# Threshold attention and routed attention on one core: crosswise scoring of tail tiles, halved subtractions and a new list

## The chip, the core and the metric

The kernel runs on one core of a Trainium2 chip. The metric is the device time in microseconds (us) of one execution, as the median of several runs; lower is better. The engines are TensorE (PE, its weight loads PEld), VectorE (DVE), ScalarE (ACT), GpSimd (POOL) and SyncE (SP, which issues transfers). The accumulation memory that TensorE writes has eight banks.

## The reference

Two attentions stand one behind the other. The first takes 8 batches of 8 heads, 576 positions and head size 64, and keeps of each row of scores only what lies within `tau` of the row's maximum:

```python
scores = scale * np.matmul(q, k.transpose(0, 1, 3, 2))
thresh = np.max(scores, axis=-1, keepdims=True) - tau
scores = np.where(scores >= thresh, scores, -1000000000.0)
...
return np.matmul(attn, v).astype(np.float32)
```

Its output, heads side by side (512 wide), is the input of a layer of four experts. Each expert projects it to queries, keys and values of width 64, does causal attention over 576 positions, projects back to 512, and each position sums its two best experts with gate weights. Everything is float32.

## The kernel before

**Tiling.** The 576 positions are four tiles of 128 rows (`R` = 4) and a tail of 64. Heads and experts go in pairs: 32 pairs of heads, and for each of 8 batches two pairs of experts. In a pair one head lies in partitions 0 to 63 and the other in 64 to 127, so that TensorE multiplies for both at once, each in one half of its rows. A float32 operand is split into a high part and the rest (`HHL`: three products instead of one). So an operand has a copy (hi) and a subtraction (lo).

**First attention, for each pair of heads** (`load`, `prep`, `scores`, `attnv`). Keys and queries are loaded (5 and 4 transfers), transposed and split in `prep` (lines 278 to 293). For pairs 1 to 5 (`NLO`) the transposed operand goes through a buffer in SBUF, so that GpSimd can do the subtraction (`flat_lo`, line 1077). For each tile `scores` (295) makes the products (`s_both`, 1091), the row minimum (keys are scaled by a negative number) with a copy out of the banks on VectorE (`s_min`, 1103), the exponential on ScalarE (`s_exp`, 1117), the masking product with its row sum on VectorE (`s_stt`, 1120), and transposes whose results are copied to SBUF (`pt`, `pa`; `out_t`, 1186). `attnv` multiplies by the values. The tail tile of a pair holds 64 rows of each head. `s_both` scores it like any other, 128 rows per head into two pairs of banks, of which half the partitions matter, and two `s_min` on 64 partitions each put both heads into one buffer of 128 rows.

**Second attention, for each batch** (`second`, 377): projections (`proj`), values, the gate, and for each pair of experts scores, exponentials and products. Queries and keys are split with `q_hi` (1299) and `q_lo` (1302). The tail of a pair of experts is one tile already: queries stand in a block-diagonal operand (`q2d`, 1305) and `s2_tail` (1394) contracts all 128 rows, then adds the causal mask by one more matmul.

**Crossing.** `crossing` (1253) lets the two row halves of TensorE add into the same pair of banks: in the first half of the work row half r writes bank r, in the second half bank 1 - r. In between, a tiny instruction on another engine (`fence`, 1269) waits for the last matmuls of the first half, and the first matmuls of the second half wait for it. Helper `crossed` (237) makes these three tasks; projections, values and outputs use it.

**Order.** All tasks are emitted in an order that stands in the code: `ORDER` gives each task its place, `BY` the engine where several can do it (for a copy from the banks 0 is ScalarE and 1 is VectorE; for a subtraction 0 is GpSimd and 1 VectorE; for a fence 0, 1, 2 are VectorE, ScalarE, GpSimd). Each engine works its tasks in this order. `plan` (131) walks through the list with estimated durations and picks buffers, banks and filler matmuls for the start; it does not change the order.

The copies, subtractions and fences that the profile lists stand in helpers: line 996 is a copy on ScalarE, 998 on VectorE, 1000 on GpSimd, 1004 every plain subtraction, 1020 every matmul, 1010 and 1167 the transposes, 1272 and 1274 the fences, 1105 `s_min`, 1118 `s_exp`, 1122 `s_stt`.

Of the kernel before, what the change touches and what calls it, by code (L numbers as in the profile page):

```python
# [25 lines left out]
R = 4  # L26
# [17 lines left out]
QUERIES = ((0, 0, 5, 0, 0), (0, WH, 4, 0, 1), (1, 0, 5, 0, 0), (1, WH, 4, 0, 1))  # L44
# [40 lines left out]
PAD, HALF, SLOW, FILL = 700.0, 8000.0, 3.5, 107.0  # L85
# [44 lines left out]

def plan(tasks, filler):
# [5 lines left out]
    moved = port = 0.0  # L137
    order = []
    for t in sorted(tasks, key=lambda t: t.place):
        e = t.by  # L140
        ready = BEGIN
        for d in t.deps:
            ready = max(ready, d.end + (SELF if t.engines == (d.by,) else LATE if t.engines == ("POOL",) else CROSS))
# [37 lines left out]


# [28 lines left out]
def work(K):  # L211
# [66 lines left out]
    def prep(n):  # L278
        ki, qi, dk, dq, dv = LD[n]
        PREP[n] = []  # L280
        for cls, src, tiles, d, scale, f in (("kk", ki, K.kis, dk, True, "k"), ("qq", qi, K.qis, dq, False, "q")):
# [4 lines left out]
            if raw:  # L286
                a = evac(W + 80 * scale, lambda e, g=g, raw=raw, scale=scale: K.in_raw(e, raw, g, scale), m, [], [g, raw], name=f"{f}r.{n}")
                h = moved(W, lambda e, buf=buf, raw=raw: K.flat_hi(e, buf, raw), [a], [], [raw, buf], name=f"{f}h.{n}")
                o = minus(W, lambda e, buf=buf, raw=raw: K.flat_lo(e, buf, raw), [h], [raw, buf], f"{f}l.{n}")
            else:  # L290
                h = evac(W + 80 * scale, lambda e, g=g, buf=buf, scale=scale: K.in_hi(e, buf, g, scale), m, [], [g, buf], name=f"{f}h.{n}")
                o = task("DVE", t_dve(W + 60 * scale), lambda g=g, buf=buf, scale=scale: K.in_lo(buf, g, scale), [h], [], [g, buf], name=f"{f}l.{n}")
            PREP[n] += [buf, [h, o]]

    def scores(n, s):
# [81 lines left out]
    def second(b):  # L377
# [8 lines left out]
        def proj(ep):  # L386
            q2, k2, q2d = Buf("q2"), Buf("k2"), Buf("q2d")
            qs, ks = [], []
            for i, (buf, l) in enumerate(((q2, qs), (k2, ks))):
# [5 lines left out]
                l += [h, minus(S, lambda e, buf=buf, rw=rw: K.q_lo(e, buf, rw), [h], [buf, rw], f"ql.{name}")]  # L395
# [23 lines left out]
        def score(t, ep, gd):  # L419
# [96 lines left out]
    for n in range(NPR):  # L516
# [13 lines left out]
BVL = ((3, 4), (2, 1, 0))  # L530
ORDER = {
    "warm": [
        638,
    ],
    "tau": [
        1, 12, 2,
# [967 lines left out]
```

## Time and profile before

| | |
|---|---|
| median of 3 runs | 855.32 us (853.39 to 855.62) |
| the profiled execution's own time | 853.47 us |
| its span, first to last instruction | 851.7 us |
| matmuls (PE), weight loads (PEld) | 14428 each |
| instructions on VectorE, ScalarE, GpSimd | 2296, 1341, 593 |
| moved by transfers | 43.15 MB |

The profile is of one execution. "x320" is a count, "752" after a comma a mean duration in ns, "idle before" the time that the engine stood still just before these instructions, with what ended it. A busy PE is not PE at its peak, since matmuls overlap and their ends are modelled.

### The profile page before, as it was taken

How to read it: one execution, taken by the hardware profiler on the slowest of the kernel's cores; microseconds unless marked ns; L12 is line 12 of the kernel's file. 1: busy time of each engine (PE TensorE's matmuls, PEld its weight loads, DVE VectorE, ACT ScalarE, POOL GpSimd, SP SyncE). 2: the span in 40 equal slices, each digit the busy share in tenths (PEclk: the TensorE clock that was granted, in tenths of full speed). 3: DMA queues.
4: the chain of work that ended last, by engine and by line, in shares of the span. 5: the costliest groups of instructions: out<-in, count | busy, mean ns of one | idle time of the engine just before them, and what ended most of it. 6: DMA issues, size and time to landing. Idle time of an engine off the chain costs nothing. (4 is left out here: it accounts for less than half of the span.)

```text
span 851.7 us, 34826 instructions
## 1 busy us (share of the span) xinstructions
PE 819.7 (96%) x14428; PEld 768.0 (90%) x14428; DVE 759.2 (89%) x2296; ACT 647.2 (76%) x1341; POOL 309.4 (36%) x593
## 2 busy tenths in 40 slices
PE   9888999999999999999999999999999999999998
PEld 7778998899989999899989999889998899988997
DVE  6999989989889989999989999999989989899564
ACT  5988768985788768987589866887678975778465
POOL 5658324521333224433243223442244233342332
PEclk9999999999999999999999999999999999999999
DMA  5333211112131211212121321122113122120002
GB/s 125 83 77 75 58 23 39 36 29 63 36 78 33 77 42 25 63 49 54 36 67 33 82 56 32 40 59 53 34 32 90 28 56 49 37 59 2 15 12 90
DMA packets 135117, 43.15 MB, mean 51 GB/s; under 512 B 130096, under 2 KB 130096, under 8 KB 134960
## 3 DMA queue, kind: packets, MB, share of 16 engines
q1 hardware_dynamic: 133744, 40.64, 19.5%
q8 instruction: 113, 1.85, 1.0%
q10 hardware_dynamic: 1216, 0.30, 0.2%
q14 instruction: 44, 0.36, 0.1%
HBM read 31.47 MB, written 9.44 MB: 48 GB/s over the span
## 5 line engine op out<-in xcount | busy, mean ns | idle before, releaser
L1105 DVE TENSOR_SCALAR_CACHE_REDUCE e<-ps 128x576 f32<-128x576 f32 (+1 forms) x320 | 233.2, 752 | 23.3 <-PE ps L1020 16.3
L1118 ACT ACTIVATE e<-e,sm 128x576 f32<-128x576 f32 x288 | 215.6, 771 | 39.0 <-DVE e L1105 35.9
L1122 DVE SCALAR_TENSOR_TENSOR e<-e,sm,e 128x576 f32<-128x576 f32 x256 | 221.1, 881 | 4.5 <-ACT e L1118 1.6
L996 ACT ACTIVATE pt<-ps 128x640 f32<-128x640 f32 (+3 forms) x247 | 154.0, 640 | 37.8 <-PE ps L1167 25.5
L1020 PE MATMUL ps<-kk,qq 64*128 64x288 f32 x1920 | 173.5, 304 | 4.1 <-DVE e L1105 1.1
L1020 PE MATMUL ps<-pt,vm 128*64 128x128 f32 (+1 forms) x1536 | 155.8, 258 | 0.0
L1020 PEld LDWEIGHTS ps<-kk,qq 64*128 64x128 f32 x1920 | 141.3, 185 | 11.9 <-DVE e L1105 3.0
L1020 PE MATMUL ps<-pa,vm 128*64 128x128 f32 x1024 | 135.7, 275 | 3.6 <-DVE e L1105 2.6
L1167 PE MATMUL ps<-ident,e 64*128 64x64 f32 x2624 | 127.0, 226 | 10.2 <-DVE e L1105 2.2
L1020 PEld LDWEIGHTS ps<-pt,vm 128*64 128x64 f32 x1536 | 131.1, 137 | 0.0
L1167 PEld LDWEIGHTS ps<-ident,e 64*128 64x128 f32 x2624 | 108.2, 138 | 22.5 <-DVE e L1105 4.8
L1020 PEld LDWEIGHTS ps<-pa,vm 128*64 128x64 f32 x1024 | 111.9, 137 | 8.5 <-DVE e L1105 3.4
L1020 PE MATMUL ps<-x,wh 64*128 64x288 f32 x1024 | 106.1, 295 | 0.0
L1020 PEld LDWEIGHTS ps<-x,wh 64*128 64x128 f32 x1024 | 84.6, 185 | 0.7 <-DVE e L1105 0.3
L996 ACT ACTIVATE pa<-ps 128x512 f32<-128x512 f32 x112 | 66.2, 593 | 17.4 <-PE ps L1167 16.5
L1020 PE MATMUL ps<-x,wl 64*128 64x288 f32 x512 | 79.1, 292 | 0.0
L1392 ACT ACTIVATE e<-e,sm 128x384 f32<-128x384 f32 (+3 forms) x128 | 71.0, 557 | 5.2 <-DVE sm L1387 5.0
L1412 POOL TENSOR_SCALAR e<-e,sm 128x256 f32<-128x256 f32 (+4 forms) x107 | 64.0, 607 | 26.5 <-DVE sm L1163 7.3
L1387 DVE CUSTOM_DVE_ANT_0 e<-ps,tri 128x384 f32<-128x384 f32 (+3 forms) x128 | 58.5, 483 | 8.4 <-PE ps L1020 7.3
L1020 PE MATMUL ps<-wh,x 64*128 64x260 f32 x640 | 64.6, 283 | 0.0
L1115 POOL TENSOR_TENSOR sm<-sm 128x2 f32<-128x2 f32 (+1 forms) x69 | 24.1, 351 | 105.3 <-DVE e L1105 80.4
L1000 POOL TENSOR_SCALAR iw<-sg 128x256 f32<-128x256 f32 (+1 forms) x61 | 25.7, 430 | 97.0 <-DVE sg L1130 56.9
(158 smaller groups left out, 1687.8 us busy)
## 6 DMA issues: line engine op xcount, KB each, us to landing
vm<-in_v_dram SPq DMA_DIRECT2D x64, 128.0 KB, 2.8
out_dram<-ob SPq DMA_DIRECT2D x32, 256.0 KB, 2.4
ki<-in_k_dram SPq DMA_DIRECT2D x96, 64.0 KB, 2.5
qi<-in_q_dram SPq DMA_DIRECT2D x62, 80.0 KB, 2.5
qi<-in_q_dram SPq DMA_DIRECT2D x62, 64.0 KB, 2.4
ki<-in_k_dram SPq DMA_DIRECT2D x32, 80.0 KB, 2.5
vt<-in_v_dram SPq DMA_DIRECT2D x128, 16.0 KB, 2.2
out_dram<-ob SPq DMA_DIRECT2D x8, 128.0 KB, 2.8
```

What stands on the lines that cost most here:

```text
L996: self.nc.scalar.activation(dst, src, AF.Copy)
L1000: self.nc.gpsimd.tensor_scalar(dst, src, 1.0, 0.0, op0=ALU.mult, op1=ALU.add)
L1020: return self.nc.tensor.matmul(out, x, y, start=first, stop=last)
L1105: self.nc.vector.tensor_scalar(self.sides(sc)[rows], self.dbank(s)[rows, :, :HS], 0.0, None, op0=ALU.add, op1=ALU.min, accum_out=self.smal ...
L1115: self.nc.gpsimd.tensor_tensor(m[:, 8 + j:8 + j + n], m[:, 2 * j:2 * (j + n):2], m[:, 2 * j + 1:2 * (j + n):2], op=ALU.add)
L1118: self.nc.scalar.activation(self.row(e), self.row(sc), AF.Exp, bias=self.small(sm)[:, 2 * j:2 * j + 1], scale=-1.0)
L1122: self.nc.vector.scalar_tensor_tensor(self.row(e), self.row(sc), self.small(sm)[:, 8 + j:9 + j], self.row(e), op0=ALU.is_le, op1=ALU.mult, ...
L1167: self.nc.tensor.transpose(self.ps[:, g.slot + h, c * D:(c + 1) * D], x, self.ident[sl, sl])
L1387: self.nc.vector.tensor_tensor_reduce(self.row(p2)[:, :w], self.dbank(g)[:, j, :w], self.tri[:, SM - w:], 1.0, FAR, op0=ALU.add, op1=ALU.m ...
L1392: self.nc.scalar.activation(p, p, AF.Exp, bias=m[:, 2 * j:2 * j + 1], scale=-1.0, accum_out=m[:, 4 + 2 * j:5 + 2 * j])
L1412: (self.nc.vector if e == "DVE" else self.nc.gpsimd).tensor_scalar(p, p, x, 0.0, op0=ALU.mult, op1=ALU.add)
```

## The change

The first attention's tail gets a query operand that is block-diagonal in its last 128 columns. To get it, the second head's last 64 positions are loaded with a transfer of their own (5 query transfers for a pair instead of 4), and two memsets instead of one put zeros beside the two tails. The tail is scored crosswise (`s_tail`) into one pair of banks, and one `s_min` on 128 partitions follows. `s2_tail` becomes a crossed group too, in 64-row halves, and the mask is added in both halves. `flat_lo` and `q_lo` are issued as two halves of the columns (320 + 320 and 288 + 288). There are 48 new fences (32 `fs`, 16 `fs2t`).

The planner compares the times at which VectorE and GpSimd hold their shared port, with the last few stretches of the other engine, instead of the last one. The constants HALF and one duration differ. All of `ORDER` and `BY` is new (5034 tasks for 4896).

In the engine choices these families change most: `pt` on VectorE 31 to 43 of 288; `pt2` 15 to 21 of 112; `v2` 5 to 0; `ob` 7 to 2; `qu` 6 to 4; `zh` 7 to 13; `thr` 48 to 55; scalings `p2s` 12 to 5; `xl` 15 to 18; halves of `q_lo` of the projections 14 of 64, where it was 6 of 32 whole ones. Fences on VectorE, ScalarE and GpSimd: 26, 27, 31 to 33, 46, 53.

```diff
-QUERIES = ((0, 0, 5, 0, 0), (0, WH, 4, 0, 1), (1, 0, 5, 0, 0), (1, WH, 4, 0, 1))
+QUERIES = ((0, 0, 5, 0, 0), (0, WH, 4, 0, 1), (1, 0, 5, 0, 0), (1, WH, 3, 0, 1), (1, SM, 1, R, 1))
...
-PAD, HALF, SLOW, FILL = 700.0, 8000.0, 3.5, 107.0
+PAD, HALF, SLOW, FILL = 700.0, 6200.0, 3.5, 107.0
...
+def hit(s, a, b):
+
+    if b <= a or s - JIT >= b or s + JIT <= a:
+        return 0.0
+    p = min(1.0, max(0.0, (a - s + JIT) / (2 * JIT)))
+    return max(0.0, soft(b - s) - soft(a - s) - (b - a) * p)
...
-            more = soft(at["POOL"] - start - 200.0)
-            port = start + more + lat - 177.0
+            more = sum(hit(start, a, z - 200.0) for a, z in theirs[-6:])
+            mine.append((start, start + more + lat - 177.0))
         elif e == "POOL":
-            more = soft(port - start)
+            more = sum(hit(start, a, z) for a, z in mine[-8:])
+            theirs.append((start + more, start + more + lat))
...
+def halves(n):
+    return slice(0, n // 2), slice(n // 2, n)
...
-                o = minus(W, lambda e, buf=buf, raw=raw: K.flat_lo(e, buf, raw), [h], [raw, buf], f"{f}l.{n}")
+                o = [minus(W // 2, lambda e, buf=buf, raw=raw, c=c: K.flat_lo(e, buf, raw, c), [h], [raw, buf], f"{f}l.{n}") for c in halves(W)]
...
-        bufs = [Buf("s") for _ in range(2)]
+        bufs = [Buf("s") for _ in range(nj)]
...
-        a = pe(6 * T_S, lambda: K.s_both(bufs, qq, kk, s), [*dk, *dq], [*bufs, *dict.fromkeys((sc, ee)), sm, sg], [qq, kk], "R", kind="S", name=f"s.{n}.{s}")
-        ms = []
-        for j in range(2):
-            x = j if s < R else 0
-            ms.append(task("DVE", (782, 80), lambda j=j, x=x: K.s_min(bufs[j], scs[x], sm, x, slice(0, P) if s < R else HEADS[j]), [a], [],
-                           [bufs[j], sc, sm], name=f"min.{n}.{s}"))
-        es = [task("ACT", (773, 101), lambda j=j: K.s_exp(scs[j], sm, ees[j], j), [ms[j]] if s < R else ms, [], [sc, sm, ee], name=f"exp.{n}.{s}")
+        takes = [*bufs, *dict.fromkeys((sc, ee)), sm, sg]
+        if s < R:
+            a = pe(6 * T_S, lambda: K.s_both(bufs, qq, kk, s), [*dk, *dq], takes, [qq, kk], "R", kind="S", name=f"s.{n}.{s}")
+        else:
+            a = crossed(3 * T_S, lambda y: K.s_tail(bufs[0], qq, kk, y), [*dk, *dq], takes, [qq, kk], bufs[0], f"s.{n}.{s}")
+        ms = [task("DVE", (782, 80), lambda j=j: K.s_min(bufs[j], scs[j], sm, j), [a], [], [bufs[j], sc, sm], name=f"min.{n}.{s}") for j in range(nj)]
+        es = [task("ACT", (773, 101), lambda j=j: K.s_exp(scs[j], sm, ees[j], j), [ms[j]], [], [sc, sm, ee], name=f"exp.{n}.{s}")
...
-                l += [h, minus(S, lambda e, buf=buf, rw=rw: K.q_lo(e, buf, rw), [h], [buf, rw], f"ql.{name}")]
+                l += [h, *[minus(S // 2, lambda e, buf=buf, rw=rw, c=c: K.q_lo(e, buf, rw, c), [h], [buf, rw], f"ql.{name}") for c in halves(S)]]
...
-                a = pe(f32r(6, HS) + 260, lambda: K.s2_tail(sb, q2d, k2), ks + dd, [sb, sm, pb], [q2d, k2], name=f"s2t.{name}")
+                a = crossed(f32r(3, HS) + 60, lambda y: K.s2_tail(sb, q2d, k2, y), ks + dd, [sb, sm, pb], [q2d, k2], sb, f"s2t.{name}")
...
+    "fs": [
+        26, 124, 220, 338, 458, 603, 756, 904, 1071, 1180, 1371, 1616, 1610, 1770, 1984, 2221, 2238, 2402, 2567, 2833, 2875, 3066, 3223, 3445, 3591, 3606, 3821, 4005, 4158, 4285,
+        4410, 4598,
...
+        692, 704, 805, 823, 1279, 1291, 1493, 1506, 1883, 1896, 2020, 2036, 2599, 2604, 2649, 2656, 3201, 3218, 3264, 3274, 3818, 3838, 3964, 3976, 4408, 4421, 4568, 4580, 4862,
+        4867, 4873, 4892,
+    ],
+    "fs2t": [
+        696, 819, 1290, 1500, 1887, 2021, 2600, 2654, 3206, 3266, 3824, 3974, 4412, 4570, 4863, 4886,
...
-        for t in self.kis + self.qis:
+        for t in self.kis:
             nc.vector.memset(t[ST:, R], 0.0)
+        for t in self.qis:
+            for j in range(2):
+                nc.vector.memset(t[ST:, R - j, j], 0.0)
...
+    def s_tail(self, s, qq, kk, y):
+
+        q, k = self.kq(qq), self.kq(kk)
+        self.crossing(HHL, y, s, lambda m, r, sl, hf, first, last: self.mm(
+            self.dbank(s)[:, hf, :HS], q[sl, m[0], SM:SM + P], k[sl, m[1], hf * HS:(hf + 1) * HS], first, last))
...
-        g = self.dbank(s)
-        for hf in range(2):
-            for i, (x, y) in enumerate(HHL):
-                self.mm(g[:, hf, :HS], self.q2ds[q2d.slot][:, x], self.q2(k2)[:, y, hf * HS:(hf + 1) * HS],
-                        i == 0, hf == 0 and i == 2)
-        self.mm(g[:, 1, HS - ST:HS], self.ident_b, self.mask2, False, True)
+    def s2_tail(self, s, q2d, k2, y):
+
+        g, q, k = self.dbank(s), self.q2ds[q2d.slot], self.q2(k2)
+
+        def mm(m, r, sl, hf, first, last):
+            x = self.mm(g[:, hf, :HS], q[sl, m[0]], k[sl, m[1], hf * HS:(hf + 1) * HS], first, last and hf == 0)
+            if hf and m is HHL[-1]:
+                x = self.mm(g[:, 1, HS - ST:HS], self.ident_b[sl], self.mask2[sl], False, last)
+            return x
+        self.crossing(HHL, y, s, mm)
```

The shown lists are the places of the fences of the first tails (`fs`), and of the two halves (`s2t`) and fences (`fs2t`) of the second tails. Between the two halves of a first tail the new list has other TensorE groups for 30 of the 32 pairs (transposes, scores, projections, outputs); for pairs 0 and 1 it has none.

## Rows read from the trace of the kernel before

**Rows 1.** The page: busy times of the engines; granted clock in 40 slices.

```profile
PE 819.7 (96%) x14428; PEld 768.0 (90%) x14428; DVE 759.2 (89%) x2296; ACT 647.2 (76%) x1341; POOL 309.4 (36%) x593
...
PEclk9999999999999999999999999999999999999999
```

**Rows 2.** Busy time by engine, sixteen 20 us stretches where VectorE is fullest, summed.

```profile
sum 320.00, PE 302.04 PEld 275.74 DVE 306.25 ACT 272.67 POOL 135.78; mean PE 43.15 PEld 39.39 DVE 43.75 ACT 38.95 POOL 19.40
```

**Rows 3.** Busy time by engine, all other stretches, summed.

```profile
sum 511.70, PE 499.12 PEld 476.95 DVE 439.88 ACT 365.14 POOL 163.90; mean PE 71.30 PEld 68.14 DVE 62.84 ACT 52.16 POOL 23.41
```

**Rows 4.** Groups by shape: the minimum on VectorE, and its accumulator read on 64 partitions.

```profile
L1105 DVE TENSOR_SCALAR_CACHE_REDUCE e<-ps 128x576 f32<-128x576 f32 x256 | 185.2, 751 | 17.1 <-PE ps L1020 13.8 <-ACT v L996 0.7 <-ACT rw L996 0.3
...
L1105 DVE TENSOR_SCALAR_CACHE_REDUCE e<-ps 64x576 f32<-64x576 f32 x64 | 48.2, 754 | 6.3 <-PE ps L1020 2.4 <-ACT pt L996 0.8 <-ACT ob L996 0.6
...
L1105 DVE DVE_READ_ACCUMULATOR e<-ps 64x1 f32 x64 | 5.0, 78 | 0.0
```

**Rows 5.** Busy time of line 1105 alone, in the stretches of rows 2, summed.

```profile
sum 320.00, DVE 96.09; mean DVE 13.73
```

**Rows 6.** Groups by shape: two copies out of the banks on VectorE.

```profile
L998 DVE COPY pt<-ps 128x640 f32<-128x640 f32 x17 | 13.8, 815 | 0.7 <-PE ps L1167 0.6
...
L998 DVE COPY ob<-ps 128x512 f32<-128x512 f32 x7 | 4.8, 688 | 3.7 <-PE ps L1020 3.4 <-issue 0.4
```

**Rows 7.** The masking product: group by shape, then its line's ns min/median/max.

```profile
L1122 DVE SCALAR_TENSOR_TENSOR e<-e,sm,e 128x576 f32<-128x576 f32 x256 | 221.1, 881 | 4.5 <-ACT e L1118 1.6 <-ACT sm L1113 0.8
...
L1122 DVE SCALAR_TENSOR_TENSOR e<-e,sm,e x256: 777/813/2185, 15.6 to 788.7; 128x576 f32<-128x576 f32 x128
```

**Rows 8.** Groups by shape: subtractions on GpSimd.

```profile
L1004 POOL TENSOR_TENSOR q<-rw,q 128x576 fp32r<-128x576 f32 x14 | 21.3, 1521 | 13.8 <-DVE sm L991 13.2 <-ACT q L996 0.4
...
L1004 POOL TENSOR_TENSOR x<-iv,x 128x256 fp32r<-128x256 f32 x21 | 16.7, 798 | 5.9 <-ACT x L996 3.6 <-DVE x L998 1.9
...
L1004 POOL TENSOR_TENSOR qq<-pt,qq 128x640 fp32r<-128x640 f32 x5 | 8.7, 1750 | 6.2 <-ACT qq L996 6.0
```

**Rows 9.** Order of time on TensorE: a second tail, then one tile's scores.

```profile
139.60 1.26 PE L1167 MATMUL ps<-ident,e 64*128 64x64 f32 x28
140.78 1.06 PE L1020 MATMUL ps<-k,q2d 128*128 128x288 f32 x6
...
141.82 0.78 PE L1167 MATMUL ps<-ident,e 64*128 64x64 f32 x18
...
406.23 0.97 PE L1020 MATMUL ps<-kk,qq 64*128 64x288 f32 x12
407.02 0.44 PE L1020 MATMUL ps<-x,wh 64*128 64x288 f32 x4
```

**Rows 10.** Fences: the group on VectorE, who waited for line 1274, one in time.

```profile
L1274 DVE TENSOR_SCALAR fenceDVE<-eps 128x2 f32<-128x2 f32 x26 | 6.4, 246 | 1.9 <-PE ps L1020 1.6
...
  PEld ps L1020: 1.8, 3
  PE ps L1020: 0.6, 2
...
704.62 0.69 DVE L1274 TENSOR_SCALAR fenceDVE<-eps 128x2 f32<-128x2 f32 x1
```

**Rows 11.** Loads: SyncE's longest wait in total, then the start in order of time.

```profile
SPq L1023 <- PE ps L1010: 206.2, 37, 18.8
...
0.80 3.50 ACTq L1023 DMA_DIRECT2D qi<-in_q_dram  x4
...
6.48 0.77 PE L1010 MATMUL ps<-ident,qi 64*128 64x64 f32 x10
7.07 0.49 PE L1010 MATMUL ps<-ident,ki 64*128 64x64 f32 x10
```

**Rows 12.** Who waited for the minimum, line 1105 (us, times).

```profile
  PEld ps L1020: 7.4, 18
  PEld ps L1167: 4.8, 13
```

More of the change, by code (lines that the diff above doesn't have):

```diff
@@ L136, in plan @@
     mode = kind = None
-    moved = port = 0.0
+    moved = 0.0
+    mine, theirs = [], []
     order = []
@@ L142, in plan @@
         for d in t.deps:
-            ready = max(ready, d.end + (SELF if t.engines == (d.by,) else LATE if t.engines == ("POOL",) else CROSS))
+            ready = max(ready, d.end + (SELF if d.by == e else LATE if e == "POOL" else CROSS))
         now = max(at[e], ready)
@@ L865 @@
-    "iw": "001001101001111002000002000120000022112000001101000001101000210200100002010000021001120002000000",
-    "iv": "0000000000001000001100001110101011001000011100000000000000100001",
-    "xh": "1121001200100101000002020020000200000102000000000110111000002210",
-    "xl": "0001000101001001010001110000000001000001000000000001001000001001",
+    "wh": "11000110000111",
+    "wl": "00000000000000",
+    "kh": "00100100000000110010000000000010",
+    "kl": "0000000001100000000000000000000000000",
@@ L869 @@
+    "iw": "000111112111211000000002010012001000100010011000021110000110101210010010221111000201220010011010",
+    "iv": "0000000010110000100010010000001001110000100000000000000000111101",
+    "xh": "0101111110101122120220111000001001101120001021120101111100011102",
+    "xl": "0001001010000111000001101000000000001000001000110000110100000011",
     "kr": "00000",
     "qr": "00000",
-    "fpj": "10211211221101122100021200002210",
-    "qu": "00100000000001000000000011001001",
-    "qd": "11102220110010010120100101100010",
@@ L880 @@
-    "fo": "212021012000011210202102210022002212",
-    "ob": "000100000000000001000000000101011100",
+    "fpj": "21222221112212121210121201102000",
+    "qu": "00100000000010000000000001000100",
+    "qd": "00000001010001011001120011212010",
+    "fv": "1012122201120211",
+    "v2": "0000000000000000",
+    "shr": "11101000100101110001110111101111101101110101101111110010010000100111111111111111",
+    "p2s": "000000000000000000210000011000022202000020010000002002000020020000000000200200000000000000000000000002020022002000000020022200000012200000000002",
@@ L882 @@
+    "pt2": "1000100010100000000010000100000001000000000000000000010001000010010000000000000010110000010000001010001001011000",
+    "fs2t": "1122120212222212",
+    "zh": "001010010010001000110100100000000000000010101010",
+    "fo": "022111200000111120111200220102200210",
+    "ob": "000000000000000000010000000000000010",
 }
@@ L1096, in s_both, with s_min @@
                 for j, sl in enumerate(HEADS):
-                    o = t * P if t < R else SM - j * ST
-                    self.mm(self.dbank(s[j])[:, hf, :HS], q[sl, x, o:o + P], k[sl, y, hf * HS:(hf + 1) * HS], i == 0, i == 2)
+                    self.mm(self.dbank(s[j])[:, hf, :HS], q[sl, x, t * P:(t + 1) * P], k[sl, y, hf * HS:(hf + 1) * HS], i == 0, i == 2)
+    def s_tail(self, s, qq, kk, y):
+        q, k = self.kq(qq), self.kq(kk)
+        self.crossing(HHL, y, s, lambda m, r, sl, hf, first, last: self.mm(
+            self.dbank(s)[:, hf, :HS], q[sl, m[0], SM:SM + P], k[sl, m[1], hf * HS:(hf + 1) * HS], first, last))
     def s_max(self, s, sm):
         self.nc.vector.tensor_reduce(self.small(sm)[:, :1], self.dbank(s)[:, :, :HS], axis=AX.XY, op=ALU.min)
-    def s_min(self, s, sc, sm, j, rows):
-        self.nc.vector.tensor_scalar(self.sides(sc)[rows], self.dbank(s)[rows, :, :HS], 0.0, None, op0=ALU.add, op1=ALU.min,
-                                     accum_out=self.small(sm)[rows, 2 * j:2 * j + 1])
+    def s_min(self, s, sc, sm, j):
+        self.nc.vector.tensor_scalar(self.sides(sc), self.dbank(s)[:, :, :HS], 0.0, None, op0=ALU.add, op1=ALU.min,
+                                     accum_out=self.small(sm)[:, 2 * j:2 * j + 1])
     def s_thr(self, e, sm, js):
```

177 lines of the change are left out of this document (82 added, 95 removed), and 269 rows, old and new, of the table ORDER.

## The prediction

> **What bounds the kernel now.** I read the page's busy lines first [rows 1]. TensorE shows 96% and its weight loads 90%, VectorE 89%, ScalarE 76%, GpSimd 36%. The reader is to see that two engines are close to full and that neither covers the span alone: VectorE stands idle for 851.7 - 759.2 = 92.5 us, so some other engine ends the waits there. Next I cut the span into stretches of 20 us and sorted them by VectorE. In sixteen of them, 320 us together (20 to 100, 140 to 180, 320 to 380, 520 to 560, 580 to 600, 640 to 680 and 740 to 780), VectorE is busy for 306.25 us, 95.7%, while TensorE has 94% [rows 2]. In the other 511.7 us it is reversed: TensorE 499.1 us, 97.5%, VectorE 439.9 us, 86% [rows 3]. So the bound changes sides within each batch: where scores of the first attention are dense VectorE sets the pace (37.6% of the span), where projections and second attention are dense TensorE does. A microsecond taken from VectorE counts in the first kind of stretch, one taken from TensorE in the second. The granted clock is nine tenths or more of full speed (2.4 GHz) in every slice [rows 1], so no term below is a clock term.
>
> **The change, part by part.**
>
> *Tail scores in one pair of banks.* The minimum on VectorE runs over 576 columns and takes as long on 64 partitions (754 ns) as on 128 (751 ns) [rows 4]. The tail tile now takes two of the first kind, after the change one of the second. That removes 32 instructions and their accumulator reads: (48.2 + 5.0) / 2 = 26.6 us of VectorE. On the path lies what falls into the VectorE stretches: the minimum is busy there for 96.09 us [rows 5], and 32 of its 320 instructions are a tenth of that: **9.6 us**. The ends are 0 (TensorE bounds everywhere) and 26.6.
>
> *Work handed to VectorE.* The new engine choices give VectorE 18 more transposed-probability copies (31 + 15 become 43 + 21, at 0.7 us [rows 6]: +12.6 us), 7 more fences (+1.7 us at 246 ns [rows 10]) and take from it 12 other copies (value 5, output 5, projection 2, at 0.69 us [rows 6]: -8.3 us). The smaller lists, counted in the same way, add about 4 us. Net +10 us, so VectorE's busy time should fall by 16 us or so before contention. Spread evenly, 37.6% of the 10 us or 3.8 us would hurt; the ends are 0 and 10. VectorE has 71.8 us idle in the other stretches [rows 3], seven times what is added, and copies can be placed there: I take **0**, with that idle as the cover and 3.8 us as the price if the copies fall evenly.
>
> *Second tail in halves of the rows.* It is now six matmuls of 128 x 288 and one of the mask: 1.04 us from 140.78 to the next group at 141.82; the last transpose before it (226 ns) began at 140.63, so entering costs 0.15 us more [rows 9]. Afterwards these are six pairs of 64-row matmuls, which start 0.79 us / 6 = 0.132 us apart [rows 9], and two mask steps of some 0.06 us (a transpose pair, also 64 columns, takes 0.78 us / 9 = 0.09 at most): 0.91 us, with no change of the array's form. 16 x 0.28 = 4.5 us of TensorE; 60% of the span is TensorE's: **2.7 us**, between 0 and 4.5. The first tail keeps its twelve matmuls, so it costs TensorE nothing more.
>
> *Subtractions halved.* The masking product on VectorE takes 813 ns in the median, 881 in the mean and up to 2185 [rows 7]; 256 x 68 ns = 17.4 us are waiting counted as busy, and the long cases are as long as GpSimd's subtractions: 1521 ns for q (k is alike), 1750 for qq [rows 8]. I give half of the 17.4 us to those, as no view splits it. From 798 ns at 256 columns and 1521 at 576 a half of 288 takes about 870 ns, so a product that runs into one waits some 57% as long at worst; I take half of 8.7 us, 4.3 us of VectorE, and 37.6% of it on the path: **1.6 us**, between 0 and 17.4 x 0.376 = 6.5 were the new list to avoid all of it. GpSimd works about 0.2 us longer per subtraction, 35 x 0.2 = 7 us of an engine with 64% idle, and its 22 more fences lie there too. The Trainium skill (SBUF — State Buffer, "Who interferes with whom") says that whichever of the two engines starts first holds the shared port for its whole instruction and the other stands still; the 2185 ns agrees. By that rule alone each half could catch a product of its own, and the term would be 0 instead of 1.6 us.
>
> *Banks.* Weight loads wait 7.4 + 4.8 us for the minimum to free banks [rows 12]. Tails are 64 of its 320 instructions and half of them go: 12.2 x 0.2 x 0.5 = **1.2 us**, between 0 and 12.2.
>
> *48 new fences.* Each crossed group has a fence that waits on TensorE in another engine's in-order queue, and TensorE's own queue waits for it. The kernel has 84 already; behind the 57 on GpSimd and VectorE weight loads and matmuls waited 1.8 + 0.6 us [rows 10]: 0.04 us each, 2.0 us for 48. That is the price with other TensorE groups between the halves. In the new list all but pairs 0 and 1 have such a group between the two halves of the first tail, and all sixteen of the second; the smallest is one group of transposes. Pairs 0 and 1 have none: 2 x 0.69 us, what the fence at 704.62 took [rows 10]. Together **-3.4 us**; the ends are 0 and 48 x 0.69 = 33. What stands behind a waiting fence: on GpSimd thresholds, inverses and subtractions, on ScalarE exponentials and copies, on VectorE the next minimum.
>
> *Loads.* Each pair has one query load more. SyncE waits 206 us for transposes to free buffers in all [rows 11], so 31 more issues are covered there; without that cover they would cost what ScalarE's take, 0.88 us each. For pair 0 ScalarE issues them, four in 3.50 us [rows 11]; the first transposes start at 6.48 and the fifth load can delay them by 0.88 us, but keys are transposed at 7.07, 0.6 us later, anyway: **-0.5 us**, between 0 and -0.9. One memset more costs nothing beside the loads.
>
> *The new list.* No row shows what another order costs. The idle of the bounding engine limits it: 13.75 us of VectorE in its stretches, 12.6 us of TensorE in the others [rows 2, 3]. I take 0 and keep these ends in the range.
>
> Sum: 9.6 + 0 + 2.7 + 1.6 + 1.2 - 3.4 - 0.5 = 11.2 us. The profiled execution took 853.47 us (span 851.7 and 1.8 around it): 842.3. The median of the three runs, 855.32, is 1.85 above it, so in its terms 844.1, say 844.
>
> **Rivals.** *VectorE bounds throughout.* For it: 95.7% in its stretches, and weight loads that wait for its banks elsewhere [rows 2, 12]. Then 26.6 - 10 + 4.3 = 20.9 us of VectorE count, less 3.9 for fences and loads: 17.0, so 855.3 - 17.0 = 838.3; with the 10 us placed in its idle, 828.3. Against: 71.8 us of idle in the TensorE stretches. *TensorE bounds throughout.* For it: 97.5% in 60% of the span. Only 4.5 + 1.2 - 3.9 = 1.8 us come off: 853.5. Against: where VectorE has 95.7%, TensorE's share drops. The Trainium skill (Perfetto Trace Analysis, "Identifying the Most-Contended Engine") judges TensorE by its weight loads' busy share, here 90% against VectorE's 89%, and so names TensorE by one point; hanging on that sentence, VectorE's freed 26.6 us would be nearly hidden. *TensorE waits at each new fence* (the side of slower). Its place is the second half of a tail at the head of TensorE's queue while the fence stands behind a long instruction, as at 704.62 [rows 10]. At 0.69 us for 48: 33 us against gains of 15.1 less 0.5, so 855.3 + 18.4 = 873.7. It decides from 14.6 / 48 = 0.30 us a fence; the present ones show 0.04. That the change is not carried out can be left aside: the two minima become one in the code.
>
> **How the numbers follow.** Forecast (838 to 851) 0.55, VectorE throughout 0.20, TensorE throughout 0.15, fences 0.10. Differences within 0.3% (2.6 us) can hardly be told from none. Faster: nearly all of the first two and a part of the third, 0.78; same 0.12; slower 0.10. The range goes from 830, most of the second rival, to 854, the third; the fences and the extreme of the second are left out, some 0.2.
>
> **What would show it.** Minimum: 288 instructions, all on 128 partitions, some 26 us less busy. VectorE's busy time near 738 us (759.2 - 26.6 + 10 - 4.3). TensorE rows of 128 x 288 gone. Mean of the masking product below 860 ns, its maximum nearer 1.7 us. TensorE's and its loads' waits on fences below 5 us in all. I would be wrong if VectorE fell by 20 us and the span by under 3, if waits on fences passed 14 us, or if the VectorE stretches became denser and no shorter.

## The result and the profile after

The changed kernel takes 829.65 us in the median (828.8 to 830.3 in four runs), the kernel before 855.47 in the same session: a ratio of 0.9691, with an interval of 0.9652 to 0.973. The gain is 25.8 us, more than twice the 11.2 forecast, and the time lies just below the low end of the range, 830. The profiled execution took 830.07 us. The prediction has no term for the granted clock; by estimate some 2 us of the gain go with it. In most of its runs beside the experiments the kernel before had a mean clock of 0.995 to 0.999 of 2.4 GHz (median 853.6 us in the six runs at 0.999, 855.4 in the fourteen at 0.995), the changed kernel 1.000 in all four. The profiled executions, at 0.999 and 1.000, are 23.3 us apart in span.

The page of the changed kernel: span, busy times by engine, granted clock in 40 slices, and the shares of the chain that ended last.

```profile
span 828.4 us, 35094 instructions
...
PE 809.9 (98%) x14537; PEld 766.2 (93%) x14537; DVE 722.7 (87%) x2263; ACT 655.0 (79%) x1389; POOL 284.0 (34%) x605
...
PEclk9999999999999999999999999999999999999999
...
PE 48%; ACT 4%; DVE 3%; issue 1%; POOL 1%; ACTq 0%; DVEq 0%; POOLq 0%
```

Set beside [rows 1], TensorE stands idle for 828.4 - 809.9 = 18.5 us where it was 851.7 - 819.7 = 32.0, and its modelled busy time is 9.8 us shorter. VectorE lost 36.5 us of work, more than the span did, so it now stands idle for 105.7 us instead of 92.5. In the waits list, TensorE's matmuls waited 20.3 us for VectorE before and wait 6.3 now; the minimum's part of that went from 8.3 to 4.0, so most of it is other work of VectorE. The two engines take turns less than before: the sixteen 20 us stretches in which VectorE is fullest are now these, summed.

```profile
sum 320.00, PE 312.18 PEld 292.39 DVE 301.65 ACT 274.81 POOL 116.53; mean PE 19.51 PEld 18.27 DVE 18.85 ACT 17.18 POOL 7.28
```

In the same number of stretches VectorE had 306.25 and TensorE only 302.04 [rows 2]. Even where VectorE is fullest, TensorE now has 97.6% (94.4% before). By these shares VectorE hardly sets the pace anywhere.

Next, the groups by shape that answer to [rows 4], [rows 7] and [rows 9], with the minimum now at line 1139, the masking product at 1156, every matmul at 1049:

```profile
L1139 DVE TENSOR_SCALAR_CACHE_REDUCE e<-ps 128x576 f32<-128x576 f32 x288 | 209.6, 753 | 25.9 <-PE ps L1049 21.5 <-ACT pt L1025 0.5 <-ACT pa L1025 0.5
...
L1156 DVE SCALAR_TENSOR_TENSOR e<-e,sm,e 128x576 f32<-128x576 f32 x256 | 207.2, 827 | 3.8 <-ACT e L1152 2.1
...
L1139 DVE DVE_READ_ACCUMULATOR e<-ps 128x1 f32 x288 | 23.8, 83 | 0.0
...
L1049 PE MATMUL ps<-k,q2d 64*128 64x288 f32 x192 | 20.2, 306 | 0.0
```

The minimum has 288 instructions, all on 128 partitions, as announced. With its accumulator reads (20.9 us on 128 partitions before, beside [rows 4]) it went from 259.3 to 233.4 us: 25.9 less. The masking product fell from 221.1 to 207.2 us, 13.9 less where 4.3 were forecast; its longest case is now 1532 ns instead of 2185:

```profile
L1156 DVE SCALAR_TENSOR_TENSOR e<-e,sm,e x256: 780/814/1532, 13.1 to 767.1; 128x576 f32<-128x576 f32 x128
```

All other work on VectorE together grew by 25.9 + 13.9 - 36.5 = 3.3 us, not 10; in it, the 32 masking products of the tails became 2.7 us shorter (28.7 to 26.0).

Last, who waited for the fences on VectorE and GpSimd, line 1308 (86 of them), in us and times:

```profile
  POOL sm L1149: 6.6, 1
  PEld ps L1049: 1.0, 2
  PEld ps L1039: 0.7, 1
  PE ps L1049: 0.5, 1
```

and for those on ScalarE, line 1306 (46):

```profile
  PEld ps L1049: 0.3, 1
  PE ps L1049: 0.2, 1
```

TensorE and its loads waited 2.7 us for all 132 fences, 0.02 us each; below 5, as announced. GpSimd's fences wait long for TensorE (138.4 us in the waits list, 83.5 before), on an engine with 66% idle.

### The profile page after: what moved, and what is told of

It reads as the page before. It is cut to its first block, busy times and chain, and to the rows that moved or that the text cites. A ratio compares the mean times of both kernels' runs of the same rounds, so it can differ in the third digit from the quotient of the medians.

```text
span 828.4 us, 35094 instructions
## 1 busy us (share of the span) xinstructions
PE 809.9 (98%) x14537; PEld 766.2 (93%) x14537; DVE 722.7 (87%) x2263; ACT 655.0 (79%) x1389; POOL 284.0 (34%) x605
## 4 chain that ended last, share of the span: by engine, by line
PE 48%; ACT 4%; DVE 3%; issue 1%; POOL 1%; ACTq 0%; DVEq 0%; POOLq 0%
PE ps L1049 39%; PE ps L1201 5%; PE ps L1039 4%; ACT e L1426 1%; DVE e L1139 1%; DVE e L1156 1%; ACT pa L1025 1%; ACT pt L1025 1%; ACT e L1152 1%; DVE e L1421 1%; POOL e L1449 0%; DVE sm L1135 0%; ACT ob L1025 0%; DVE z L1033 0%; ACT e L1441 0%
## 5 line engine op out<-in xcount | busy, mean ns | idle before, releaser
L1139 DVE TENSOR_SCALAR_CACHE_REDUCE e<-ps 128x576 f32<-128x576 f32 x288 | 209.6, 753 | 25.9 <-PE ps L1049 21.5
L1156 DVE SCALAR_TENSOR_TENSOR e<-e,sm,e 128x576 f32<-128x576 f32 x256 | 207.2, 827 | 3.8 <-ACT e L1152 2.1
L1049 PE MATMUL ps<-kk,qq 64*128 64x288 f32 x1920 | 176.5, 304 | 3.8 <-DVE e L1139 1.4
L1025 ACT ACTIVATE pt<-ps 128x640 f32<-128x640 f32 (+3 forms) x236 | 148.4, 643 | 26.5 <-PE ps L1201 16.0
L1049 PEld LDWEIGHTS ps<-x,wh 64*128 64x128 f32 x1024 | 86.5, 185 | 0.6 <-issue 0.2
L1426 ACT ACTIVATE e<-e,sm 128x256 f32<-128x256 f32 (+3 forms) x128 | 70.8, 556 | 4.5 <-DVE sm L1421 4.1
L1025 ACT ACTIVATE pa<-ps 128x512 f32<-128x512 f32 x105 | 62.1, 593 | 10.4 <-PE ps L1201 9.5
L1421 DVE CUSTOM_DVE_ANT_0 e<-ps,tri 128x256 f32<-128x256 f32 (+3 forms) x128 | 58.8, 485 | 10.8 <-ACT v L1025 6.5
L1308 POOL TENSOR_SCALAR fencePOOL<-eps 128x2 f32<-128x2 f32 x53 | 14.9, 281 | 151.3 <-PE ps L1049 138.4
L1049 PE MATMUL ps<-woh,z 64*128 64x256 f32 x512 | 59.1, 293 | 0.3
```

Source lines behind the costliest of these rows:

```text
L1025: self.nc.scalar.activation(dst, src, AF.Copy)
L1049: return self.nc.tensor.matmul(out, x, y, start=first, stop=last)
L1139: self.nc.vector.tensor_scalar(self.sides(sc), self.dbank(s)[:, :, :HS], 0.0, None, op0=ALU.add, op1=ALU.min, accum_out=self.small(sm)[:, ...
L1156: self.nc.vector.scalar_tensor_tensor(self.row(e), self.row(sc), self.small(sm)[:, 8 + j:9 + j], self.row(e), op0=ALU.is_le, op1=ALU.mult, ...
L1308: g.fence = eng.tensor_scalar(self.fences[e], self.eps, 1.0, 0.0, op0=ALU.mult, op1=ALU.add)
L1421: self.nc.vector.tensor_tensor_reduce(self.row(p2)[:, :w], self.dbank(g)[:, j, :w], self.tri[:, SM - w:], 1.0, FAR, op0=ALU.add, op1=ALU.m ...
```

## The experiments

Times are medians; "in place" means at the position that the list gives the task. Most variants keep the buffers of the kernel that they start from, so that the edit alone differs; where buffers were planned anew, it is said. The edits are shortened, and some of their lines tell in words what changes.

### The old list with all the new work, and the new list with all the old work

The first takes the code of the changed kernel and the places and engine choices of the kernel before, the new tasks put in by a rule; the second takes the new list and undoes the three edits of the work, except that the first tail stays crossed, with its fence, in one pair of banks.

```diff
-ORDER, BY = (new)
+ORDER, BY = (old)
+ORDER["s"]: first half where the tail stood, fence behind it, second half behind 0.6 us of other groups
+ORDER["min"]: the one minimum at the later of its two old places
```

> The list and the buffers of the kernel before, with all three edits of the work put into it by a rule: the first half of a tail where the tail stood, its fence (ScalarE and GpSimd in turn) right behind, the second half behind 0.6 us of other TensorE work, the one minimum where the later of the two stood, both halves of a subtraction in the place of the whole one. Theory W (the removed work brings the gain): VectorE falls by 26 us and the time to 833 to 842. Theory L (the new list brings it, above all by keeping the masking product clear of GpSimd): the mean of the masking product stays near 860 ns or above and the time is 845 to 853. If fences that nobody planned for hold TensorE: over 856.

885.54 us, a ratio of 1.035 (1.0323 to 1.0378): 30 us slower than before, though VectorE has 26 us less to do (733.0). The waits list shows a part of where it went; the first is a weight load, the second a matmul waiting for a fence on ScalarE:

```profile
PEld ps L1149 <- ACT fenceACT L1406: 8.3, 12, 1.9
...
PE ps L1149 <- ACT fenceACT L1406: 6.4, 12, 1.8
```

The second run's edit is the three diffs of the next section together (two minima, the second tail in 128 rows, whole subtractions).

> The new list, with the old work in it: the tail's minimum as two instructions on 64 partitions each (from the one pair of banks, which crossing still fills), the second tail as 128-row matmuls, whole subtractions at the place of the earlier half. Theory W: back to 850 to 858, since all of the removed work is there again. Theory L: masking product still under 840 ns, time 835 to 845.

859.34 us, 1.0058 (1.0038 to 1.0078): the list alone loses some 4 us. The masking product's mean nevertheless fell to 832 ns, with whole subtractions of 1444 ns on GpSimd: the new list, not the halving, does most to keep the two engines out of each other's way. That alone buys no time, and TensorE waits longer for the minimum than in the kernel before (37.0 us against 18.3, in the four kinds of waits shown in the next section).

```profile
L1240 DVE SCALAR_TENSOR_TENSOR e<-e,sm,e 128x576 f32<-128x576 f32 x256 | 208.5, 832 | 4.1 <-ACT e L1236 2.3 <-ACT fenceACT L1390 0.2
```

So the gain is neither the work's nor the list's alone. The next runs take the edits one by one.

### One part undone under the new list

**The minimum** as two instructions on 64 partitions, as in the run above:

```diff
-        ms = [task("DVE", ..., lambda j=j: K.s_min(bufs[j], scs[j], sm, j), [a], ...) for j in range(nj)]
+        ms = ... if s < R else [task("DVE", ..., lambda j=j: K.s_min(bufs[0], scs[0], sm, 0, HEADS[j]), [a], ...) for j in range(2)]
```

> The changed kernel with one part undone: each tail's minimum as two instructions on 64 partitions, which puts 26.6 us back on VectorE and nothing else. By the forecast's share of stretches in which VectorE is the bound: 829.7 + 9.6 = 839. If VectorE bounds throughout (theory W at its full size): 829.7 + 26 = 856. If TensorE bounds throughout: 830 to 832.

847.87 us, 0.9918 (0.9898 to 0.9938): 18.2 us lost for 26.4 us more on VectorE (749.1). The chain has 24% of TensorE and 6% of VectorE, and TensorE waits for the minimum to free banks (lines 1123 and 1275 are its matmuls and transposes):

```profile
PEld ps L1123 <- DVE e L1213: 12.5, 25, 1.1
PEld ps L1275 <- DVE e L1213: 9.0, 18, 1.1
PE ps L1123 <- DVE e L1213: 7.6, 21, 0.9
...
PE ps L1275 <- DVE e L1213: 5.5, 10, 0.9
```

The same four lines of the changed kernel:

```profile
PEld ps L1049 <- DVE e L1139: 4.2, 10, 1.2
...
PEld ps L1201 <- DVE e L1139: 4.1, 12, 0.8
...
PE ps L1201 <- DVE e L1139: 1.7, 5, 0.6
...
PE ps L1049 <- DVE e L1139: 1.4, 5, 0.3
```

34.6 us against 11.4 (loads and matmuls may wait at the same time): VectorE's work counts as banks that come free late. But the kernel before, with the same 320 minima in a list made for them, waited much less than this run:

```profile
PEld ps L1020 <- DVE e L1105: 7.4, 18, 2.1
PEld ps L1167 <- DVE e L1105: 4.8, 13, 1.0
PE ps L1020 <- DVE e L1105: 3.9, 8, 1.9
...
PE ps L1167 <- DVE e L1105: 2.2, 5, 0.8
```

That is 18.3 us. So some 16 of the 34.6 us are a misfit, waits that the same minima do not cause in a list made for them, and the 18.2 us lost are likely more than what removing the second minimum brought; by how much, no run shows. Sixteen of the fullest stretches of this kernel, summed, look as those of the kernel before did, with 306.25 and 302.04 [rows 2]:

```profile
sum 320.00, PE 305.02 PEld 281.95 DVE 306.65 ACT 270.99 POOL 124.07; mean PE 19.06 PEld 17.62 DVE 19.17 ACT 16.94 POOL 7.75
```

So with as many stretches as full as before (320 of 846.1 us, 37.8%), 18.2 of 26.4 us count here, 69%, with the misfit in it.

**The subtractions** whole again, at the place of the earlier half:

```diff
-                o = [minus(W // 2, ..., c=c: K.flat_lo(e, buf, raw, c), ...) for c in halves(W)]
+                o = [whole(W, lambda e, ...: K.flat_lo(e, buf, raw, slice(0, W)), ...)]
```

> The changed kernel with whole subtractions at the place of the earlier half. Forecast's term: 1.6 us, so 831. If halving is what cleared the port (masking product 881 to 827 ns, 14 us of VectorE): the mean goes back above 860 ns and the time to 835 to 843. If the list alone cleared it: mean under 840 ns and 829 to 832.

833.15 us, 0.9742 (0.9722 to 0.9762): 3.5 us, of which VectorE's busy time shows 3.8 (726.5); the longest masking product is 2072 ns again.

**The second tail** with 128 rows, at the place of its second half, and in another run at the place of its first half:

```diff
-                a = crossed(f32r(3, HS) + 60, lambda y: K.s2_tail(sb, q2d, k2, y), ...)
+                a = pe(f32r(6, HS) + 260, lambda: K.s2_tail(sb, q2d, k2), ...)
```

> The changed kernel with the second tail as before (six 128-row matmuls and the mask, at the place of the second half, no fence). Forecast's term: 2.7 us, so 832.5. If the parts add up to what separates the new list with the old work from the changed kernel (859.3 - 829.7 = 29.6, of which the minimum 18.2 and the halves 3.5): 829.7 + 7.9 = 837.6.

> The changed kernel with the second tail as before, this time at the place of the first half. The run with it at the place of the second half lost 9.0 us, of which TensorE's own stream explains about 4 (4.5 us in the forecast). If the rest is that the maximum behind it came later: 829.7 + 4.5 = 834. If the changes of form cost it: 838 to 839 again.

838.69 us, 0.9808 (0.9789 to 0.9827), and 839.39 us, 0.9812 (0.9786 to 0.9838): 9.0 and 9.7 us, so the place is not the point. In order of time on TensorE, first a second tail of the changed kernel with its halves, then one of the first variant:

```profile
114.67 0.57 PE L1049 MATMUL ps<-k,q2d 64*128 64x288 f32 x6
...
115.08 1.10 PE L1201 MATMUL ps<-ident,e 64*128 64x64 f32 x26
115.99 0.64 PE L1049 MATMUL ps<-k,q2d 64*128 64x288 f32 x6
...
116.48 0.80 PE L1049 MATMUL ps<-kk,qq 64*128 64x288 f32 x8
```

```profile
116.40 1.05 PE L1123 MATMUL ps<-k,q2d 128*128 128x288 f32 x6
...
117.43 0.80 PE L1123 MATMUL ps<-kk,qq 64*128 64x288 f32 x8
```

The halves hold TensorE for 0.41 + 0.49 = 0.90 us (0.91 was forecast), the whole tail for 1.03 and the entry: the tail's own cost was sized rightly, 4.5 us at most for sixteen. The other half of the 9 us is spread over TensorE; idle is 2.2 us more (836.7 - 816.0 = 20.7 against 18.5).

**The first tail** in 128 rows as well, one minimum as in the changed kernel, no fence:

```diff
-            a = crossed(3 * T_S, lambda y: K.s_tail(bufs[0], qq, kk, y), ...)
+            a = pe(6 * T_S, lambda: K.s_wide(bufs[0], qq, kk), ...)
```

> The changed kernel with the first tails scored by six matmuls over all 128 rows (the block-diagonal queries) at the place of the first half, instead of twelve crossed ones and a fence: one minimum as before, 32 more changes of the array's form on entering and on leaving, 32 fences fewer. If a change of form costs what sixteen second tails showed (9.0 and 9.7 us, so 0.56 to 0.6 us a tail): 847 to 850 us. If it costs only the 0.15 us on entering and the slower matmuls (0.28 us a tail): 837 to 840 us. If the fences that go pay for it: 828 to 832 us.

844.37 us, 0.9866 (0.9843 to 0.989): 14.7 us, 0.46 a tail, between the two expectations. Such a tail, from 38.28 to 39.26, takes 0.98 us (rows below); twelve crossed matmuls take 0.79 [rows 9]. So in this list the block-diagonal operand alone would be a poor way to save the minimum; scoring crosswise is worth its fence.

```profile
38.28 1.05 PE L1123 MATMUL ps<-kk,qq 128*128 128x288 f32 x6
39.26 0.53 PE L1113 MATMUL ps<-ident,qi 64*128 64x64 f32 x10
```

### The same parts done under the old list

**The subtractions** halved, nothing else; then **the wide tail** with one minimum, at the later of the old places, at the earlier, and with two minima at both.

```diff
-        self.minus(self.kq(buf)[:, 1], self.pt(raw), self.kq(buf)[:, 0], e)
+        for c in (slice(0, W // 2), slice(W // 2, W)):
+            self.minus(self.kq(buf)[:, 1, c], self.pt(raw)[:, c], self.kq(buf)[:, 0, c], e)
```

> The kernel before with its long subtractions (keys and queries) issued as two halves at the same place, nothing else. Forecast's term: 1.6 us, so 853.4; by the new list's loss without halves 3.5 us, so 851.5. Mean of the masking product from 881 to about 855 ns if halving alone clears the port; if two halves in a row hold it as long as a whole one, 875 or more and no change of time.

```diff
-        a = pe(6 * T_S, lambda: K.s_both(bufs, qq, kk, s), ...)
+            a = pe(6 * T_S, lambda: K.s_wide(bufs[0], qq, kk), ...)
+    ORDER["min"]: max(m[:2]), then min(m[:2]), then both places m[:2] with two minima
```

> The list and buffers of the kernel before; the first tail is scored into one pair of banks without crossing: six 128-row matmuls against the block-diagonal queries, then one minimum. So VectorE loses 26.6 us without any fence, and TensorE gains two changes of form per tail (32 x 0.3 = 9.6 us). If the removed minimum counts as in the new list (18.2 us) and the changes of form for 60%: 855 - 18.2 + 5.8 = 842.6. If only a list made for it can use the time: 850 to 856.

> As the old list with the wide tail (866.9 us), but the one minimum of a tail stands at the earlier of its two old places instead of the later. If the later place hid the minimum's worth under the old list: 848 to 858 us. If the old list cannot use the freed VectorE time wherever it falls: within 3 us of 866.9. If the earlier place makes VectorE wait on TensorE's matmuls: above 870, with longer waits of the minimum on TensorE.

> The old list with the 128-row tail of the run before, but the minimum again as two instructions of 64 partitions at their two old places. Against that run (866.9) it has the 26.6 us of VectorE back and nothing else, so the difference is what the removed minimum is worth under the old list. If worth as much as under the new list: 866.9 + 18.2 = 885. If the old list leaves the freed time unused: 867 to 872.

| under the old list | us | ratio to before | VectorE busy |
|---|---|---|---|
| halved subtractions | 852.47 | 0.9966 (0.9946 to 0.9985) | 757.9 |
| wide tail, one minimum, later place | 866.9 | 1.0135 (1.0112 to 1.0159) | 736.3 |
| wide tail, one minimum, earlier place | 867.47 | 1.0153 (1.0138 to 1.0168) | 737.8 |
| wide tail, two minima | 870.13 | 1.0169 (1.0142 to 1.0195) | 761.0 |

Halving brings 3.0 us, close to the 3.5 under the new list; the masking product's mean fell only to 870 ns, its longest case to 1546. The 24.7 us of VectorE that separate the second row from the fourth bring 3.2 us, little more than the spread of the runs, where under the new list they brought 18.2. The four waits of TensorE for the minimum sum to 17.3 us with one minimum and to 19.0 with two (18.3 in the kernel before). Where the one minimum stands makes no difference, so its later place did not hide its worth: with these tails the old list does not use the time. One rival is left: the wide tails themselves make this list 11 us slower, and crossed tails with one and with two minima were not set side by side under it.

### Is it the engine choices, the order, or the buffers?

Only the engine choices of the 23 families that both kernels have in equal number are exchanged, in both directions (555 of these 1454 tasks change their engine); then the planner's formula, also both ways (here buffers and banks are planned anew, and order and choices stay).

```diff
-BY["pt"], BY["pt2"], BY["thr"], BY["p2s"], ... = (one kernel's)
+BY["pt"], BY["pt2"], BY["thr"], BY["p2s"], ... = (the other's)
```

> The changed kernel with its work, its order and its buffers, but the old engine choices for every family that is not new (copies, thresholds, scalings, hi copies; 23 families, 12 copies out of the banks of the second kind fewer on VectorE). Order theory (the new order is what lets freed VectorE time count): near the changed kernel, 830 to 836 us, VectorE about 10 us less busy. Choices theory (the copies given to VectorE shorten the path to TensorE): most of the gain goes, 845 to 860 us, with weight loads waiting longer for copies on ScalarE. Third: the choices fit their own order alone, so both of this pair of runs are worse than their base by over 5 us.

> The kernel before with its work, order and buffers, and the new engine choices for the same 23 families. Choices theory: faster than before, 840 to 850 us. Order theory: 853 to 860 us. Third (choices fit their own order alone): 860 us or more.

937.22 us, 1.096 (1.0932 to 1.0988), and 958.29 us, 1.1207 (1.1186 to 1.1228). Each set of choices costs over 100 us in the other's order. VectorE's busy time changes little (732.7 for 722.7, and 756.4 for 759.2), but TensorE stands idle for 937.4 - 850.2 = 87.2 and 956.0 - 856.0 = 100.0 us. Waits of the first of the two on copies of transposed probabilities, where the changed kernel's loads at line 1049 waited 3.4 us:

```profile
PEld ps L1121 <- ACT pt L1097: 14.4, 25, 1.8
...
PE ps L1121 <- ACT pt L1097: 10.2, 15, 1.6
```

The order stands for the choices and the choices for the order; in these two exchanges neither shows a worth of its own.

```diff
-            more = sum(hit(start, a, z - 200.0) for a, z in theirs[-6:])
+            more = soft(at["POOL"] - start - 200.0)
```

> The changed kernel with the old port formula and constants in the planner, so that only buffers and banks can come out differently; work, order and engine choices stay. If the new formula matters to the emitted kernel: 835 us or more, with longer waits for banks. If it served only to find the list: within 1.5 us of 829.7.

> The kernel before with the new port formula and constants in its planner: work, order and engine choices stay, only buffers and banks are chosen anew. If the new formula estimates the times better for any list, so that buffers come free in time: 846 to 852 us. If buffers fit the formula that the list was made with: slower than before, 858 to 868 us, with longer waits for banks, as the changed kernel lost 9.5 us with the old formula. If the choice hardly matters under the old list: within 2 us of 854.9.

839.12 us, 0.9816 (0.9801 to 0.9831), and 856.15 us, 1.0007 (0.9993 to 1.0022). With the same order and choices, other buffers and banks alone (and the fillers of the start that go with them) cost the changed kernel 9.5 us, with waits of TensorE for the minimum again (7.2 + 4.9 us at its first two lines, 4.2 + 1.4 in the changed kernel). The kernel before gains nothing from the new formula.

```profile
PEld ps L1047 <- DVE e L1137: 7.2, 14, 1.6
...
PE ps L1047 <- DVE e L1137: 4.9, 10, 1.4
```

### The fences, the port and what VectorE is still worth

**Fences with nothing between the halves**: the first half and the fence of all 48 new crossed tails are moved right in front of the second half.

```diff
+        a.place = b.place - 0.2
+        x.place = b.place - 0.1
```

> The changed kernel with the first half and the fence of all 48 new crossed tails moved directly ahead of the second half, so that TensorE has nothing between them. If a fence costs little however it is placed: under 836. If it costs TensorE what the stalled ones of the old list with the new work cost (26.7 us in 44, 0.6 us each): 829.7 + 48 x 0.6 = 858. A new fence is then cheap only because the list puts work between the halves.

877.2 us, 1.0274 (1.0237 to 1.0311): 47.5 us more than the changed kernel, 1.0 us a fence. The three kinds of fence in the waits of weight loads:

```profile
PEld ps L1128 <- POOL fencePOOL L1387: 17.9, 25, 2.3
...
PEld ps L1128 <- ACT fenceACT L1385: 8.0, 14, 1.0
...
PEld ps L1128 <- DVE fenceDVE L1387: 5.2, 8, 0.9
```

**Each halved subtraction issued twice** on GpSimd:

```diff
-                 fn
+                 lambda e: [fn(e) for _ in range(2 if e == "POOL" else 1)]
```

> The changed kernel with every halved subtraction on GpSimd issued twice (the same result written twice), so that GpSimd holds the shared port for some 56 us more. If the port matters: masking product's mean up by 20 ns or more, VectorE's waiting in it by 5 us or more, time 834 to 840. If GpSimd's chain is what counts, the product's mean stays below 835 ns and the time still rises. If neither: 830 to 831.

853.95 us, 0.9983 (0.9967 to 0.9999), above the 834 to 840 expected for the port: 24.3 us for 62 us of GpSimd, an engine that was 34% busy. VectorE's busy time grew by 10.8 us (733.5), the masking product to 849 ns; before it VectorE now waits 4.4 us for GpSimd's thresholds (group by shape):

```profile
L1230 DVE SCALAR_TENSOR_TENSOR e<-e,sm,e 128x576 f32<-128x576 f32 x256 | 212.9, 849 | 10.3 <-POOL sm L1223 4.4 <-ACT wh L1099 2.4 <-ACT e L1226 2.0
```

**Less of VectorE still**: 32 small multiplications left out.

```diff
-            l = task("DVE", t_dve(ST + 100), lambda: K.x_tail(g, iv, w), ...)
+            l = task("DVE", t_dve(ST + 100), lambda: None, ...)
```

> The changed kernel without the small multiplication that scales the second head's tail rows (32 instructions of 228 ns on VectorE, 7.3 us; those rows come out scaled by the first head's sum). If a microsecond of VectorE still counts 18.2 / 26.6 = 0.68 going down: 829.7 - 5.0 = 824.7. If the changed kernel is bound by TensorE, so that VectorE's time counts only when it is added: 829 to 830.

829.22 us, 0.9696 (0.9671 to 0.9722): 9.2 us off VectorE (713.5) bring 0.4 us, no more than the spread of the runs. In the changed kernel these 9.2 us no longer count, while 26.4 us put back cost 18.2.

## Why the prediction was wrong in size

**The direction and the mechanisms held.** The announced signs came, but for one: the minimum's count and its 25.9 us, no rows of 128 x 288 in the second tail, a masking product below 860 ns in the mean with a longest case of 1532, fence waits of 2.7 us. VectorE's busy time came to 722.7 us instead of 738, as the masking product gave 13.9 us and the handed work took 3.3. None of the signs that would have made it wrong appeared. What failed are sizes, and for the most part they failed by one step.

**The failing step: "On the path lies what falls into the VectorE stretches."** A part's microseconds were multiplied with the share of the span that its engine bound under the old list. So 26.6 us of minimum, 4.5 of second tail and 4.3 of masking product, 35.4 together, became 9.6 + 2.7 + 1.6 = 13.9. Undone under the new list, the three parts cost 30.7 us one by one and 29.7 all at once, more than twice that, and the change as a whole brought 25.8 us where 11.2 were forecast. The shares told how the old list spends its time; the list made anew with the shorter work was not bound by them. How the 25.8 us divide among the parts is less sure. For the minimum, priced at 9.6, the runs give 18.2 with a misfit in it, and 3.2 under the old list with wide tails; no run prices it alone in a list made for it. The rival "VectorE bounds throughout" was nearer in number: its 838.3, or 828.3 with the 10 us hidden, brackets the result. Its reason, that weight loads wait for VectorE's banks outside the stretches [rows 12], fits what TensorE's waits show.

**Banks: 1.2 us.** The prediction counted the waits of two kinds of weight loads for the minimum, 12.2 us, and took a tenth. Those two fell to 4.2 + 4.1 = 8.3, by 3.9 us; with the matmuls the four fell from 18.3 to 11.4. And TensorE's matmuls wait for more of VectorE than its minimum: 20.3 us before, 6.3 after. This term was too small, and the waits for the rest of VectorE had none.

**"The new list: 0."** As a term of a sum this can't be given. The list with most of the old work is worth -4 us, the new work put into the old list by a rule -30, and both together +25.8. The three parts undone singly lose 18.2 + 9.0 + 3.5 = 30.7 us, all three at once 859.34 - 829.65 = 29.7: under the new list they add up, so what is missing is a list term of about -4, not an interaction of the parts. Exchanging choices alone costs over 100 us, buffers alone 9.5, so a list fits only what it was made with. This cuts both ways: each "undone" run also carries a misfit, so 18.2 and 9.0 are what undoing the part costs in this list, not the saving of its instructions alone. The minimum's waits (34.6 us there, 18.3 in the kernel before) show that the misfit is not small. Its size stays open; no list made anew for a single part was run.

**Second tail: 2.7, measured 9.0 and 9.7.** Its own time on TensorE was right (0.90 us a tail for 0.91). The step that took 60% of 4.5 us because the rest lay where VectorE set the pace made the term too small: TensorE is now busy for 98% of the span, which fits the whole 4.5 counting. The remaining half shows only as 2.2 us more idle and as more busy time elsewhere on TensorE. Its cause isn't settled; a misfit may be in it as well.

**Halves: 1.6, measured 3.5 and 3.0.** The two lists agree, so this is a part with a worth of its own, inside the bounds of 0 to 6.5. The Trainium skill (SBUF — State Buffer, "Who interferes with whom") has either engine hold the shared port for its whole instruction; the longest case with whole subtractions (2072 ns) and with halves (1532) agrees with that. The zero that the rule alone would have allowed, each half catching a product of its own, did not come.

**Work handed to VectorE: 0, and +3.3 us instead of +10.** That it cost no time fits its cover, the idle time. Of the 6.7 us by which it came out smaller, 2.7 are the shorter masking products of the tails; the rest is spread over small groups.

**Fences: -3.4, and the slower rival.** The price of a covered fence held (2.7 us of waits for 132). So did the rival's condition: with nothing between the halves 1.0 us a fence, above the 0.69 that it assumed, and in the old list, where the rule left 0.6 us between the halves by estimate, fences held TensorE (8.3 + 6.4 us of waits in the rows above) and so had a part in losing 30 us. What decided against that rival was the list.

**TensorE throughout: 853.5.** After the change TensorE does bound nearly throughout (98%, and 9.2 us less of VectorE no longer count), but it is a state that the change brought, not one that it found. The Trainium skill (Perfetto Trace Analysis, "Identifying the Most-Contended Engine") judges TensorE by the work that it does as a share of its peak and by its weight loads' busy share. The second was 90% before and is 93% after; by that the kernel before would have been TensorE's already and the freed VectorE time nearly hidden. The measurement decides against this rival: 829.65 us, not 853.5. Under the old list with wide tails, where 24.7 us of VectorE brought 3.2, it would have been nearly right.

## What to carry to other kernels

Where two engines near 90% wait for each other through a few banks, don't price a microsecond taken from one by the share of time in which it is full: here savings of 35.4 us, priced at 13.9, came with a gain of 25.8 once the schedule was remade, and in the old schedule the largest of them brought 3 us. Judge an edit and its schedule together, and read the waits for banks beside the busy shares. An edit undone in a schedule that was made for it costs more than it brought, so set its waits beside those of the kernel before. A hand-over between row halves through another engine is nearly free with other TensorE work in between (0.02 us of waits each here) and costs about 1 us without.

## What the runs showed that was not expected

Exchanging the engine of 555 copies, subtractions, fences and small steps, in an order that was written for other choices, cost 103.4 us in one direction and 107.6 in the other, several times any edit of the work. Choosing other buffers and banks for the very same instructions in the same order cost 9.5 us under the new list and 0.9 (within its interval) under the old. An engine that is busy for 34% of the span is no free place: doubling 62 us of subtractions on GpSimd lost 24.3 us, nearly the gain of the whole change. In the two runs with exchanged choices, where TensorE idled most, its mean granted clock was 0.982 and 0.978 of 2.4 GHz, against 1.000 and 0.999 in the kernels that they start from.
